# Decay constants made on GpSimd, pair 0 split first, masks beside layer 1, and a new order in pairs 4 to 8 of a fused attention and MLP kernel

## The chip, the cores and the metric

The kernel runs on one core of one Trainium2 chip. The metric is device time in microseconds, taken as the median of the timed runs. Times inside the kernel come from one execution that the hardware profiler recorded; they count from the start of its span.

## The reference

Eight batches of eight heads, 576 tokens, head size 64. Each head is causal attention with a decay that is built from a running sum of `s`. The heads of a batch are then put side by side and go through a two-layer MLP with a hard-swish.

```python
scores = (1/8) * q @ k.T                        # per batch and head, 576 x 576
cum    = cumsum(maximum(s, 0), axis=-1)
bias   = -(cum[:, :, :, None] - cum[:, :, None, :])
scores = where(causal, -1e9, scores + minimum(bias, 0))
attn   = softmax(scores)                        # over the last axis
x      = (attn @ v) -> (8*576, 8*64)            # 4608 tokens x 512
h      = x @ w_in                               # 512 x 2048
out    = (h * clip(h + 3, 0, 6) / 6) @ w_out    # 2048 x 512, float32
```

## The kernel before

**Pairs of heads.** The 64 heads are worked in 32 pairs; four pairs are a batch. A pair's q and k are cast to float16 and transposed into `qT` and `kT`, three slots deep (`NS = 3`, slot is pair modulo 3). Rows 0 to 63 hold the head dimension. Rows 64 to 67 hold the decay: the running sum split in three float16 parts (high, middle, low) on the k side, and its negative on the q side, with ones across from them. So one matmul gives scores and decay together. The remaining rows of a slot, up to 127, hold constant mask rows, which are written once per slot. They make the later pairs' scores causal at a coarse grain.

**Batch 0 (pairs 0 to 3, `FIRST = 4`)** has a start-up path of its own. `first_columns` takes `s` in 128 pieces of 64 tokens, scans each (`scan`), and lets TensorE add up the pieces with two selection matrices, `sums`, which are loaded from DRAM. The split parts go straight into the spare columns of `x0`, a tile of q and k rows in float16, and `turn_first` transposes 68 columns at once. `scores_half` computes half of a head's scores over all 128 rows and adds the triangle with matmuls on `ident` and `tri`. `keep_warm` issues matmuls that compute nothing. The mask rows of slot 0 are made by `affine_select` on GpSimd and copied into slots 1 and 2 by VectorE (`mask_rows`), all within batch 0.

**Layer 1 of block 0.** The MLP works in nine blocks of 512 tokens. `m1` is the first layer (four matmuls of 512 columns for each of 16 f tiles, then ScalarE and VectorE), `m2` the second (four parts of four matmuls for each of four token tiles t4). While layer 1 of block 0 runs, `decay_scan` and `decay_rows` make the decay rows for all other heads. `store_aug` writes them to DRAM scratch and `load_aug` brings a pair's four rows into its slot of `qT` and `kT`.

**The queue of SP.** Nearly all loads are issued by SP, in program order. Pair 4's loads (`load_nine`, contiguous rows) stand behind a small transfer, `fence`, which reads from a part of `w_out`. So they are not issued before that part of `w_out` has landed:

```python
nc.sync.dma_start(out=fence_dram, in_=w_out_sb[0:1, 7, 0:32])
load_nine(FIRST)
```

`w_out` is loaded in four quarters of four f rows each by GpSimd's queue; row 7 is in the second quarter. Then come the loads of pairs 5 and 6, each with its aug rows.

**Layer 2 of block 0 beside pairs 4 to 8.** The 16 parts of `m2(0, ...)` are the list `fill`. Some are run before pair 4's transposes (`turn_nine`); the others are handed out, one at each `more()`, inside `second_pair`, which writes out the order of a pair's scores (`s0`, `s1`, four banks for each head), values (`v`, in two groups) and transposes by hand. From pair 9 on, `weave` mixes attention and MLP tasks by weights.

**PSUM.** Banks 0 to 2 are a ring for scores ("S"), which `x_transpose` also uses; 3 and 4 a ring for the MLP, with transposes in 3; 5 the ring "Y"; 6 and 7 hold attention outputs.

Engines run their own queues in program order. The schedule is manual: what stands first in the program is issued first on its engine.

Of the kernel before, what the change touches and what calls it, by code (L numbers as in the profile page):

```python
# [16 lines left out]
def kernel(  # L17
# [49 lines left out]
    def pair_of_banks(b):  # L67
# [4 lines left out]
    NG = COLS * W2 // 64  # L72
    g = np.arange(128)
    sel_np = g[:, None] == g[None, :NG]
    low_np = (g[:, None] < g[None, :NG]) & (g[:, None] // 9 == g[None, :NG] // 9)
    sums_dram = nc.inline_tensor(
        np.ascontiguousarray(
            np.stack([m[:, k::2] for k in range(2) for m in (sel_np, low_np)], axis=1)
        ).astype(np.float32),
        name="sums",  # L80
    )

    PARTS = [(2 * FIRST, 14), (14, 20), (20, 32), (32, 48), (48, NH)]
# [19 lines left out]
    warm = cpool.tile([128, 512], F16, tag="c_warm")  # L103
    one = cpool.tile([128, 2], F16, tag="c_one")
    keep = cpool.tile([128, 64], F16, tag="c_keep")
# [13 lines left out]
    s_first = work.tile([128, 64], F32, tag="s_first", bufs=1)  # L119
    sums = work.tile([128, 4, NG // 2], F32, tag="sums", bufs=1)  # L120
    scan = work.tile([128, 64], F32, tag="scan", bufs=1)
# [30 lines left out]
    def mask_view(sl, i):  # L152
        return (kT, qT)[i][64:128, sl, 0:W2].rearrange("p (h t) -> p h t", h=2)

    nc.vector.memset(warm, 0.0)
    nc.vector.memset(one[:, 0:1], 1.0)
    nc.vector.memset(x0[:, :, :, 0, D:D + 3], 1.0)
    nc.vector.memset(x0[:, :, :, 1, D + 3:D + 4], 1.0)
    both = [[0, 2], [1, SEQ]]
    select(  # L160
        mask_view(0, 1), both, 4 * GRAN, -GRAN, -16384.0,
        warm[64:128, 0:1].unsqueeze(1).to_broadcast([64, 2, SEQ]),
    )
    select(ident, [[1, 128]], 0, -1, 0.0, one[:, 0:1].to_broadcast([128, 128]))
    select(ident, [[-1, 128]], 0, 1, 0.0)

    def key_rows():
        nc.vector.memset(one[:, 1:2], 1.0)
        k_rows = mask_view(0, 0)
        select(  # L170
            k_rows, both, 4 * GRAN, -GRAN, 0.0,
            one[64:128, 1:2].unsqueeze(1).to_broadcast([64, 2, SEQ]),
        )
        select(k_rows, [[0, 2], [-1, SEQ]], -4 * GRAN + GRAN - 1, GRAN, 0.0)
        select(tri, [[1, 128]], 0, -1, -65504.0, warm[:, 0:128])

    def more_pads():
        nc.gpsimd.memset(kT[:, :, W2:W2 + 64], 0.0)
        nc.gpsimd.memset(v_f[64:128, :, :, 4, :], 0.0)
        nc.gpsimd.memset(v_h[:, :, :, :, D:VW], 1.0)  # L180
        nc.gpsimd.memset(Pm[:, :, 1600:PW], 1.0)
        select(keep, [[1, 64]], 0, -1, 0.0, one[:, 0:1].to_broadcast([128, 64]))

    def mask_rows(sl, i):
        nc.vector.tensor_copy(out=mask_view(sl, i), in_=mask_view(0, i))

# [217 lines left out]
    def scores_half(hd, half):  # L404
        p, hh = hd // 2, hd % 2
        sl = p % NS
        off = hh * SEQ
        b, p0, parts, masks = HALVES[half]
        S = pair_of_banks(b)
        ops = []  # L410
        for kt, lo, hi, c in parts:
            ops.append((
                c, hi - lo, kT[:, sl, off + 128 * kt:off + 128 * (kt + 1)],
                qT[:, sl, off + lo:off + hi],
            ))
        for c, n in masks:
            ops.append((c, n, ident, tri[:, 0:n]))
        ops.sort(key=lambda o: o[0] // 512)
        for i, (c, n, lhsT, rhs) in enumerate(ops):
            bk = c // 512  # L420
            nc.tensor.matmul(  # L421
                out=S[:, c:c + n], lhsT=lhsT, rhs=rhs,
                start=(i == 0 or ops[i - 1][0] // 512 != bk),
                stop=(i == len(ops) - 1 or ops[i + 1][0] // 512 != bk),
            )
        n = max(c + n for c, n, _, _ in ops)
        nc.scalar.activation(  # L427
            out=Pm[:, hd % NS, p0:p0 + n], in_=S[:, 0:n], func=AF.Exp, scale=0.125, bias=0.0
        )
# [245 lines left out]
    def second_pair(p, fill):  # L675
# [9 lines left out]
        if first:  # L685
            run(s0[2:3])
            cast_qk(p + 1)
            more()
        else:
            transpose_group(p, 1)  # L690
            before = values(2 * p - 1)
            run(before[0] + s0[2:3] + before[1])
            if p in (FIRST + 2, FIRST + 4):
                m2_result(0, (p - FIRST) // 2)
        run(s0[3:])
        if first:
            more()
            mask_late()
            run(s1[:3])
            transpose_group(p + 1, 0)  # L700
            mask_late()
            run(v[0] + v[1] + s1[3:])
        else:
            cast_qk(p + 1)
            mask_late()
            run(s1[:2])
            more()
            x_transpose(p - 1)
            run(s1[2:3] + v[0] + s1[3:])
            transpose_group(p + 1, 0)  # L710
            mask_late()
            run(v[1])
        load_aug(p + 3, nc.sync)
# [66 lines left out]
    def first_columns():  # L780
# [5 lines left out]
        )  # L786
        key_rows()
        cT = PS[:, 7, 0:NG // 2]
        for half in range(2):
            o = cT[64 * half:64 * half + 64, :]  # L790
            nc.tensor.matmul(
                out=o, lhsT=scan, rhs=sums[:, 2 * half, :], start=True, stop=False
            )
            nc.tensor.matmul(
                out=o, lhsT=scan[:, 63:64].to_broadcast([128, 64]), rhs=sums[:, 2 * half + 1, :],
                start=False, stop=True,
            )
        c3 = cT.rearrange("p (a t) -> p a t", a=COLS)
        r3 = rest.rearrange("p (a t) -> p a t", a=COLS)
        hi, mid, lo = (x0[:, :, :, 1, D + j] for j in range(3))  # L800
        nc.vector.tensor_copy(out=hi, in_=c3)
        nc.scalar.activation(out=x0[:, :, :, 0, D + 3], in_=hi, func=AF.Copy, scale=-1.0)
        nc.vector.tensor_tensor(out=r3, in0=c3, in1=hi, op=ALU.subtract)
# [3 lines left out]
    def cast_first(p, i, t0, t1, copy):  # L807
        copy(out=x0[:, p, t0:t1, i, 0:D], in_=qk_f[p][:, t0:t1, i, :])

    def turn_first(p, i, t0, t1, b, copy):  # L810
        pT = f16(pair_of_banks(b) if (t1 - t0) > 8 else PS[:, b, :], (t1 - t0) * 128)
        for t in range(t0, t1):
            c = (t - t0) * 128
            nc.tensor.matmul(
                out=pT[0:XW, c:c + 128], lhsT=x0[:, p, t, i, :], rhs=ident,
                is_transpose=True, start=(c % 1024 == 0),
                stop=(t == t1 - 1 or c % 1024 == 896),
            )
        dst = (qT, kT)[i]
# [6 lines left out]
    load_part(0, 0, 0, 5, A)  # L826
    A.dma_start(out=sums, in_=sums_dram.ap())
    load_part(0, 1, 0, 5, nc.sync)
# [7 lines left out]

    keep_warm(7)
    cast_first(0, 0, 0, 5, A.copy)
    cast_first(0, 1, 0, 5, A.copy)
    first_columns()  # L840
    keep_warm(2)
    turn_first(0, 0, 0, 5, 4, A.copy)
    turn_first(0, 1, 0, 5, 5, V.tensor_copy)
    cast_first(0, 0, 5, 9, G.tensor_copy)
    cast_first(0, 1, 5, 9, G.tensor_copy)
    mask_rows(1, 1)
    keep_warm(1)
# [11 lines left out]
    for hd in range(2 * FIRST):  # L859
        p, odd = hd // 2, hd % 2  # L860
        scores_half(hd, 0)
        if hd == 0:
            turn_first(0, 0, 5, 9, 6, V.tensor_copy)
            turn_first(0, 1, 5, 9, 7, V.tensor_copy)
            mask_rows(1, 0)
        if not odd:
            if p == 0:
                cast_pair(1)
                more_pads()
            if p == 2:  # L870
# [12 lines left out]
        elif p + 1 < FIRST:  # L883
            turn_first(p + 1, 1, 0, 9, 4, V.tensor_copy)
            if p + 2 < FIRST:
                cast_pair(p + 2)
        scores_half(hd, 1)
        if hd > 0:
            attend(hd - 1)
        if hd == 1:  # L890
            for i in range(2):
                mask_rows(2, i)
        if odd and p > 0:
# [19 lines left out]
    store_aug(0)  # L913
    nc.sync.dma_start(out=fence_dram, in_=w_out_sb[0:1, 7, 0:32])
    load_nine(FIRST)
    load_aug(FIRST, nc.sync)
    load_v(FIRST, nc.sync)
    for p in range(FIRST + 1, FIRST + 3):
        load_pair(p)
        load_aug(p, nc.sync)  # L920
    store_aug(1)
    run(m1_0[5:14])
    m2_of = {n: m2_tasks(n) for n in range(NBLK)}
    run(m1_0[14:])
    cast_nine(FIRST)
    cast_v(FIRST)
    parts = [(0, 0), (0, 1), (0, 2), (1, 0), (1, 1), (0, 3), (1, 2), (1, 3)]
    parts += [(t4, part) for t4 in (2, 3) for part in range(4)]
    fill = [(lambda t4=t4, part=part: m2(0, t4, part, t4 == 3), 1.0) for t4, part in parts]
    run(fill[:3])  # L930
    turn_nine(FIRST, 6)
    run(fill[3:6])
    m2_result(0, 0)
    fill = fill[6:]
    second_pair(FIRST, fill)
    for p in range(FIRST + 1, PXD + 1):
        second_pair(p, fill)
    ph = PS[:, 4, :]
    m1_sum(1, 0, ph, range(KC - 1))
    transpose_group(PXD + 1, 1)  # L940
    m1_sum(1, 0, ph, range(KC - 1, KC))
    m1_act(1, 0, ph)
    def weighted(m1s, m2s):
        return [(task, 0.85) for task, _ in m1s] + [(task, 1.3) for task, _ in m2s]

    weave(att_of[0], weighted(m1_tasks(1)[1:], m2_of[1][:12]))
    second = weighted([], m2_of[1][12:]) + weighted(m1_tasks(2), m2_of[2][:8])
# [39 lines left out]
```

## Time and profile before

| what | value |
|---|---|
| timed runs | 355.48, 355.26, 352.92 us; median 355.26 us |
| profiled execution, its own time | 352.95 us |
| profiled execution, its span | 351.2 us |
| PE busy | 342.0 us (97%) |
| DVE, ACT, POOL busy | 203.2, 207.0, 147.2 us |
| DMA | 53.99 MB, mean 154 GB/s |
| granted TensorE clock | 1.00 |

PE is TensorE, DVE VectorE, ACT ScalarE, POOL GpSimd, SP SyncE; PEld is the load of weights into TensorE. A line of the timeline gives the start, the duration, the engine, the line of the program, the operation, output <- inputs, and in brackets how long the engine had been idle and who released it. A line of the chain gives start, duration and what it was. Matmul ends are modelled: a 512-column matmul is recorded with 379 ns, while one follows the other by 216 ns.

### The profile page before, as it was taken

The page shows a single profiled execution, that of the slowest core. Times are in us where ns is not written, and L with a number is a line of the kernel's source. Part 1 is how long each engine was busy: PE and PEld are TensorE (multiplying, and loading weights), DVE is VectorE, ACT ScalarE, POOL GpSimd, SP SyncE. Part 2 cuts the span into 40 slices and gives each one's busy share as a digit, 9 for nine tenths or more (in the row PEclk, how much of TensorE's full clock was granted, in tenths as well). Part 3 has the DMA queues.
Part 4 walks back from the last instruction along what each step waited for, and adds up shares of the span by engine and source line. Part 5 has one row for each costly group of instructions (what it writes and reads, how often), then busy time and mean ns, then how long its engine had stood idle before and what let it go on. Part 6 is the DMA issues. An engine that isn't in the chain of part 4 may idle for free.

```text
span 351.2 us, 7616 instructions
## 1 busy us (share of the span) xinstructions
PE 342.0 (97%) x2797; PEld 199.3 (57%) x2797; DVE 203.2 (58%) x367; ACT 207.0 (59%) x392; POOL 147.2 (42%) x318
## 2 busy tenths in 40 slices
PE   7999799999999999999999999999999999999996
PEld 3775366666555655555555555555565545444444
DVE  3758567887635883566546644756365635644531
ACT  3776547678655885777467755775577615534410
POOL 7884157654556455545545444444444200000000
PEclk9999999999999999999999999999999999999999
DMA  8999999999999988988897789787923110010012
GB/s 180 240 164 215 220 214 209 199 243 183 175 197 233 207 169 185 210 196 135 200 197 169 157 185 209 151 175 171 219 40 84 49 60 32 17 45 30 30 60 91
DMA packets 160415, 53.99 MB, mean 154 GB/s; under 512 B 152410, under 2 KB 154266, under 8 KB 160378
## 3 DMA queue, kind: packets, MB, share of 16 engines
q1 hardware_dynamic: 157178, 48.68, 63.1%
q0 software_dynamic: 2256, 4.46, 6.8%
q8 instruction: 22, 0.36, 0.5%
q10 hardware_dynamic: 944, 0.37, 0.4%
q14 instruction: 15, 0.12, 0.1%
HBM read 37.47 MB, written 9.95 MB: 135 GB/s over the span
## 4 chain that ended last, share of the span: by engine, by line
PE 85%; DMA 8%; SPq 2%; POOL 2%; DVE 1%; ACT 1%; issue 0%; POOLq 0%
PE PS L565 34%; PE PS L522 31%; PE PS L346 11%; PE PS L443 7%; DMA w_out_sb<-in_moe_w_out_dram 4%; DMA qkf<-in_k_dram 3%; DMA v_f<-in_v_dram 1%; PE PS L591 1%; SPq L200 1%; PE PS L297 1%; DVE qkT L312 1%; ACT Pm L353 1%; POOL v_h L294 1%; SPq L214 0%; SPq L881 0%
## 5 line engine op out<-in xcount | busy, mean ns | idle before, releaser
L522 PE MATMUL PS<-xT,w_in 128*128 128x512 f16 x576 | 142.3, 379 | 0.0
L533 DVE SCALAR_TENSOR_TENSOR gT<-trl,PS 128x512 f16<-128x512 f32 x144 | 97.8, 686 | 76.8 <-ACT trl L532 76.4
L532 ACT ACTIVATE trl<-PS,bias 128x512 f32<-128x512 f32 x144 | 98.8, 693 | 72.7 <-PE PS L522 72.1
L565 PE MATMUL PS<-w_out_sb,gT 128*128 128x512 f16 x560 | 138.7, 379 | 0.0
L353 ACT ACTIVATE Pm<-PS 128x384 f16<-128x384 f32 x224 | 101.5, 509 | 46.8 <-PE PS L346 44.0
L358 POOL TENSOR_SCALAR_AFFINE_SELECT Pm<-Pm 128x64 f16<-128x64 f16 (+2 forms) x214 | 70.6, 333 | 112.4 <-ACT Pm L353 103.3
L522 PEld LDWEIGHTS <-w_in 128*128 128x128 f16 x576 | 60.4, 114 | 44.2 <-issue 0.2
L565 PEld LDWEIGHTS <-gT 128*128 128x128 f16 x560 | 51.0, 98 | 48.5
L346 PE MATMUL PS<-qkT 128*128 128x256 f16 x392 | 61.7, 261 | 1.2 <-DVE qkT L312 0.7
L346 PEld LDWEIGHTS <-qkT 128*128 128x128 f16 x392 | 35.9, 98 | 30.3 <-DVE qkT L312 3.4
L443 PEld LDWEIGHTS <-Pm 128*128 128x128 f16 x960 | 37.7, 97 | 11.1
L443 PE MATMUL PS<-v_h,Pm 128*128 128x65 f16 x960 | 41.0, 193 | 0.0
L580 DVE TENSOR_SCALAR osb<-PS 128x512 f32<-128x512 f32 x34 | 23.4, 688 | 28.5 <-PE PS L565 28.5
L460 DVE TENSOR_TENSOR xs<-PS,r 128x640 f16<-128x640 f32 (+1 forms) x37 | 27.2, 734 | 1.3
L278 POOL CAST xb<-qkf 128x1152 f16<-128x1152 f32 x22 | 25.5, 1159 | 0.0
L294 POOL CAST v_h<-v_f 128x640 f16<-128x640 f32 x32 | 24.0, 750 | 1.9 <-DMA v_f<-in_v_dram 1.9
L427 ACT ACTIVATE Pm<-PS 128x896 f16<-128x896 f32 (+1 forms) x16 | 13.1, 836 | 4.4 <-PE PS L421 4.4
L289 DVE COPY qkT<-turned 64x1152 f16<-64x1152 f16 x22 | 10.6, 482 | 7.1 <-DMA turned<-xb 7.1
L459 DVE RECIPROCAL r<-PS 128x10 f32<-128x10 f32 (+1 forms) x37 | 7.8, 211 | 7.9 <-PE PS L443 7.3
L290 DVE COPY qkT<-turned 64x1152 f16<-64x1152 f16 x22 | 10.9, 496 | 0.3
L312 DVE COPY qkT<-PS 64x640 f16<-64x640 f16 (+1 forms) x20 | 9.1, 453 | 2.8 <-PE PS L297 2.7
L421 PE MATMUL PS<-qkT 128*128 128x64 f16 (+4 forms) x48 | 9.0, 277 | 0.6 <-DVE qkT L820 0.4
(71 smaller groups left out, 112.5 us busy)
## 6 DMA issues: line engine op xcount, KB each, us to landing
out_dram<-osb SPq DMA_DIRECT2D x35, 256.0 KB, 2.8
qkf<-in_q_dram SPq DMA_DIRECT2D x31, 288.0 KB, 3.5
qkf<-in_k_dram SPq DMA_DIRECT2D x31, 288.0 KB, 4.2
v_f<-in_v_dram SPq DMA_DIRECT2D x62, 128.0 KB, 3.3
w_out_sb<-in_moe_w_out_dram POOLq DMA_DIRECT2D x4, 512.0 KB, 15.8
v_f<-in_v_dram SPq DMA_DIRECT2D x32, 32.0 KB, 2.8
w_in<-in_moe_w_in_dram POOLq DMA_DIRECT2D x2, 512.0 KB, 7.3
w_in<-in_moe_w_in_dram POOLq DMA_DIRECT2D x1, 1024.0 KB, 11.9
```

Source lines behind the costliest of these rows:

```text
L278: nc.gpsimd.tensor_copy(out=xb[:, p % 2], in_=qk_f.pop(p))
L294: nc.gpsimd.tensor_copy(out=v_h[:, sl, :, :, 0:D], in_=v_f[:, sl])
L346: nc.tensor.matmul(out=S[:, c:c + hi - lo], lhsT=kT[:, sl, off + 128 * kt:off + 128 * (kt + 1)], rhs=qT[:, sl, off + lo:off + hi], start=( ...
L353: nc.scalar.activation(out=P[:, p0:p0 + n], in_=S[:, 0:n], func=AF.Exp, scale=0.125, bias=0.0)
L358: nc.gpsimd.affine_select(out=view, in_=view, pattern=pattern, compare_op=ALU.is_ge, fill=0.0, base=0, channel_multiplier=-1,)
L443: nc.tensor.matmul(out=O[:, hh, qt * VW:qt * VW + D + 1], lhsT=P[:, c:c + 128], rhs=v_h[:, sl, hh, kt, 0:D + 1], start=(qt == 0), stop=(qt ...
L460: nc.vector.tensor_tensor(out=x_tiles[p].rearrange("p t h d -> p h t d")[:, heads], in0=Ov[:, :, :, 0:D], in1=r[:, 0:n].to_broadcast([128, ...
L522: nc.tensor.matmul(out=ph, lhsT=w_in_t[f // 4][:, kc, f % 4, :], rhs=xT[:, kc, n * 512:(n + 1) * 512], start=(kc == 0), stop=(kc == KC - 1),)
L532: nc.scalar.activation(out=trl, in_=ph, func=AF.Relu, bias=bias3[:, 0:1], scale=1.0)
L533: nc.vector.scalar_tensor_tensor(out=gT2[:, n % 2, f, :], in0=trl, scalar=6.0, in1=ph, op0=ALU.min, op1=ALU.mult)
L565: nc.tensor.matmul(out=po, lhsT=gT2[:, n % 2, f, t4 * 128:(t4 + 1) * 128], rhs=w_out_sb[:, f, :], start=(f == 0), stop=(f == NF - 1),)
L580: nc.vector.tensor_scalar_mul(out=osb, in0=pouts[n, t4], scalar1=1.0 / 6.0)
```

## The change

It has five parts.

- `sums` is no longer loaded; GpSimd makes it in four selects from a tile of float32 ones. GpSimd makes its own ones, and VectorE takes over the memsets of paddings.
- Pair 0 gets tiles of its own: `q0`, `k0`, and `dec0` for the decay columns of k. `split_of` splits pair 0's nine columns first and those of pairs 1 to 3 later. The k side of pair 0 is transposed in two groups, 64 columns of k and 4 of decay.
- The scores of batch 0 run over 68 rows, so mask rows are not needed there. They are made after `decay_rows`, by GpSimd in slot 2 and by a GpSimd copy into slot 1; ScalarE copies them into slot 0.
- The fence reads a row of the third quarter of `w_out`. The aug loads of pairs 5 and 6 stand behind all loads of pairs 5 and 6 and the second store of decay rows.
- In layer 2, five parts run before `turn_nine` and two after it (before: three and three). Inside a pair the parts and scores change places, and the sums of two f tiles of block 1 are started early in banks 4 and 5.

The core of the diff:

```diff
-    A.dma_start(out=sums, in_=sums_dram.ap())
+    sel, low = sums[:, 0], sums[:, 1].rearrange("p (a b) -> p a b", b=9)
+    nh = NG // 9
+    select(low, [[9, nh], [1, 9]], -1, -1, 0.0, one_f.unsqueeze(1).to_broadcast([128, nh, 9]))
+    select(low, [[-9, nh], [0, 9]], 0, 1, 0.0)
+    select(sel, [[1, NG]], 0, -1, 0.0, one_f.to_broadcast([128, NG]))
+    select(sel, [[-1, NG]], 0, 1, 0.0)
...
+    def make_masks():
+        q_rows, k_rows = mask_view(MADE, 1), mask_view(MADE, 0)
...
+        for i in (1, 0):
+            nc.gpsimd.tensor_copy(out=mask_view(FIRST % NS, i), in_=mask_view(MADE, i))
...
     def mask_rows(sl, i):
-        nc.vector.tensor_copy(out=mask_view(sl, i), in_=mask_view(0, i))
+        nc.scalar.copy(out=mask_view(sl, i), in_=mask_view(MADE, i))
...
-                c, hi - lo, kT[:, sl, off + 128 * kt:off + 128 * (kt + 1)],
-                qT[:, sl, off + lo:off + hi],
+                c, hi - lo, kT[0:XW, sl, off + 128 * kt:off + 128 * (kt + 1)],
+                qT[0:XW, sl, off + lo:off + hi],
...
-            if p in (FIRST + 2, FIRST + 4):
-                m2_result(0, (p - FIRST) // 2)
+            if p in (FIRST + 1, FIRST + 2):
+                m2_result(0, p - FIRST)
...
             mask_late()
+            more()
             run(s1[:2])
-            more()
             x_transpose(p - 1)
-            run(s1[2:3] + v[0] + s1[3:])
+            run(v[0] + s1[2:3])
             transpose_group(p + 1, 0)
             mask_late()
-            run(v[1])
+            run(s1[3:] + v[1])
...
+    def split_of(cT, a0, a1):
+        n = a1 - a0
...
+            hi, mid, lo = (dec0[:, :, j].unsqueeze(1) for j in range(3))
+            minus = q0[:, :, D + 3].unsqueeze(1)
         nc.vector.tensor_copy(out=hi, in_=c3)
-        nc.scalar.activation(out=x0[:, :, :, 0, D + 3], in_=hi, func=AF.Copy, scale=-1.0)
+        nc.vector.tensor_scalar_mul(out=minus, in0=hi, scalar1=-1.0)
...
-    keep_warm(7)
+    keep_warm(5)
...
-    first_columns()
-    keep_warm(2)
+    sums_of = first_columns()
+    split_of(sums_of, 0, 1)
+    keep_warm(1)
...
-            turn_first(0, 1, 5, 9, 7, V.tensor_copy)
-            mask_rows(1, 0)
+            turn_first(0, 1, 5, 9, 5, V.tensor_copy)
...
-            turn_first(p + 1, 1, 0, 9, 4, V.tensor_copy)
+            turn_first(p + 1, 1, 0, 9, 6 if p == 0 else 4, V.tensor_copy)
...
+    make_masks()
-    nc.sync.dma_start(out=fence_dram, in_=w_out_sb[0:1, 7, 0:32])
+    nc.sync.dma_start(out=fence_dram, in_=w_out_sb[0:1, 11, 0:32])
...
     for p in range(FIRST + 1, FIRST + 3):
         load_pair(p)
-        load_aug(p, nc.sync)
     store_aug(1)
...
+    for i in (1, 0):
+        mask_rows((FIRST + 2) % NS, i)
+    for p in range(FIRST + 1, FIRST + 3):
+        load_aug(p, nc.sync)
...
-    run(fill[:3])
+    run(fill[:5])
     turn_nine(FIRST, 6)
-    run(fill[3:6])
+    run(fill[5:7])
     m2_result(0, 0)
-    fill = fill[6:]
+    early = [m1_sum_early(f) for f in range(2)]
+    fill = fill[7:] + early
```

## The prediction

> **What bounds the kernel now.** I read the page first (busy shares, slices), then the chain of waits, the waits by length, and timelines of the stages that the diff touches.
>
> ```profile
> PE 342.0 (97%) x2797; PEld 199.3 (57%) x2797; DVE 203.2 (58%) x367; ACT 207.0 (59%) x392; POOL 147.2 (42%) x318
> DMA  8999999999999988988897789787923110010012
> ```
>
> TensorE is busy 342.0 of 351.2 us, and the DMA engines are nearly full for two thirds of the span. No matmul of the main work is removed, so the change can only fill holes in PE: 9.2 us that the page shows, plus short stalls that the modelled ends of matmuls cover. The chain says what ends last early on:
>
> ```profile
> 15.64 3.63 DMA v_f<-in_v_dram
> ...
> 22.01 14.85 DMA w_out_sb<-in_moe_w_out_dram
> 37.59 5.64 DMA qkf<-in_k_dram
> 44.69 2.59 PE PS L565 x12
> ```
>
> Up to 44 us the end is set by data, not by engines: pair loads, the second quarter of w_out (landed 36.86), then pair 4's q and k (landed 43.23), whose issue stands behind the fence on that quarter. From 44.69 on the chain is PE. Three kinds of hole lie in the changed stages, by the timeline:
>
> ```profile
> 4.88 0.44 PE L791 MATMUL PS<-sums,scan 128*64 128x36 f32 x4 [0.45 <-DMA sums<-sums]
> 16.32 0.67 POOL L808 CAST gT<-qkf 128x576 f16<-128x576 f32 x1 [0.54 <-DMA qkf<-in_q_dram]
> 19.42 0.72 POOL L294 CAST v_h<-v_f 128x640 f16<-128x640 f32 x1 [0.39 <-DMA v_f<-in_v_dram]
> 44.02 0.68 PE L297 MATMUL PS<-idtri,t 128*128 128x128 f16 x9 [1.90 <-POOL t L255]
> 58.99 0.28 PEld L346 LDWEIGHTS <-qkT 128*128 128x128 f16 x4 [0.53 <-DVE qkT L312]
> ```
>
> First, the decay columns wait for the constants `sums` until 4.88, though `scan` is done at 3.53. The casts of pair 3 and of v of pair 2 wait for their loads. Second, PE waits 1.90 us for pair 4 (42.1 to 44.0). Third, in pairs 5 to 8, the first score of the second head waits for the copies out of the second transpose group, about half a microsecond each time.
>
> **What the Trainium skill says.** "DMA: Bandwidth & Descriptors", section "Issuing engines are not separate DMA queues": transfers issued from different engines run on the same 16 DMA engines and interleave. The trace agrees: pair 4's k needs 5.64 us while the w_out stream runs, against a median of 4.2 us for k loads. Its section "Queues, rings and completion order": within a ring, descriptors are consumed in order, so a small load issued late stands behind the large ones before it; the trace records no landing for the aug loads, since nothing waited for one. "TensorE: Matmul & The Clock Gate", section "LDWEIGHTS (loading the stationary operand)": a weight load's time goes by columns, not by contraction rows. So scores over 68 rows instead of 128 gain nothing on PE. The trace has 98 ns for 128 columns at every score; no run yet shows fewer rows.
>
> **The change part by part.**
>
> *Constants by GpSimd, pair 0 split first.* A select of 64x1152 takes 1154 ns and one of 128x128 takes 296, so about 0.84 ns per element: 0.25 us for 72 columns. Float32 is not shown; I bound it at 0.5. Four of them from about 1.0 put `sums` at 2.0 (at most 3.0), before the scan's 3.53. DVE's added memsets (0.09 to 0.47 each, mostly under 0.2, by their like) fit before s_first lands at 3.0. The sum matmuls then start at 3.6, not 4.88. DVE starts 0.77 after them, at 4.4 (as 5.65 follows 4.88); five small operations (0.32, about 0.2, 0.21, 0.28, 0.32) end at 5.75. Five transposes of `dec0` (0.5) and a copy (0.49) give the first score at 6.9 instead of 8.06: PE is 1.15 us earlier. Nine extra transposes (about 0.06 each, 0.5 us) are in this; three warm matmuls go. Using banks 6 and 7 for pair 1's k also removes a 0.46 us wait.
>
> How much of it lasts? Pair 3's q cast waits for its load and ends at 16.99; its transposes run at 17.47. So the lead falls to 0.5 us there. v of pair 2 is cast at 20.14, and attention uses it at 20.31: the lead falls to 0.2. The removed 72 KB of `sums` may bring the loads 0.3 us earlier (72 KB at the 230 GB/s of that stage). I carry 0.3 us to the end of batch 0; the bounds are 0 and 1.2.
>
> *Masks beside layer 1.* Four DVE copies of mask rows (0.46 to 0.65) leave batch 0. POOL gets three selects (3 x 1.15), two copies (about 1.15 each, like the cast of 1152 elements) and `keep` after its decay rows, that is from 34.3 to about 40.5; it was idle until pair 4's cast at 42.57. ACT gets two copies (about 1.1 each by the estimate from its 1152 columns) after 40.26; it was idle until 47.48. Both are covered: 0. Without that cover pair 4's aug load would be late; it waited until 41.34 anyway, for the store of the decay rows.
>
> *The fence moves one quarter on, turning pair 4 moves behind five fills instead of three.* The issues of w_out begin at 21.48, 22.01, 22.57 and 23.1. With the view's 12.9, 15.8 (median) and 18.8 us to landing and 36.86 for the second, the landings are 34.4, 36.9, 39.3 and 41.9. Pair 4's loads are thus issued at 39.6, not 37.17. They do not lose 2.4 us: most of the bytes moved only when the stream ended. From 41.9 to 43.23 the old kernel had about half of the 576 KB left; now about three quarters are left, some 0.6 us more. I take a k landing of 43.7 (43.2 to 44.5). Cast 0.7, transposes 0.7 and hand-overs put the end of the turn at 45.15, against 44.70. But PE has then done five fills of 0.86 us instead of three: 1.73 - 0.45 = 1.3 us gained. If the transfers behave as the stream alone allows, 0.5 to 1.7. One part of it is at risk: bank 4 is needed for a fill about 3.3 us after the turn, while DVE frees it at 3.75 (four copies, 3.11, and the result's 0.67): 0.5 us, hidden by what follows.
>
> *The aug loads of pairs 5 and 6 go behind all loads of pairs 5 and 6 and a store.* This is the step that I hold against the change. SP's timeline before:
>
> ```profile
> 47.03 0.43 SPq L227 DMA_DIRECT2D qkT<-aug_scratch  x1
> 47.50 0.37 SPq L200 DMA_DIRECT2D qkf<-in_q_dram  x1
> 47.91 0.61 SPq L200 DMA_DIRECT2D qkf<-in_k_dram  x1
> 48.62 1.55 SPq L214 DMA_DIRECT2D v_f<-in_v_dram  x2
> 50.22 0.61 SPq L218 DMA_DIRECT2D v_f<-in_v_dram  x1
> 50.93 0.71 SPq L227 DMA_DIRECT2D qkT<-aug_scratch  x1
> 51.69 0.29 SPq L617 DMA_DIRECT2D aug_scratch<-aug  x1
> ```
>
> Pair 5's aug load leaves at 47.03; now it is passed by q, k and three v loads of pair 6 and the store. Take out its 0.47, add the store's 0.34: it leaves at 50.7. A landing takes 2.8 us (median of the small v loads just ahead of it in the ring; bounds 2.2, s_first with little ahead, and 4.4, the longest q load seen). So pair 5's rows are there at 53.5 (52.5 to 55.5). Pair 5's first score waits for them, and PE runs in order: all fills, values and transposes are queued behind. PE would otherwise be there at 45.15 + 6.3 (the old 7.2 from turn to pair 5, less one fill) + 0.5 = 51.9. It idles 1.6 us. In all, pair 5 starts at 53.5 with ten fills done; before, it started at 51.89 with nine. 53.5 - 51.89 - 0.86: a loss of 0.75 us, with everything gained further up swallowed. ACT and DVE idle with PE there.
>
> *Order within pairs 5 to 8.* The fill of 0.86 us moves between the last score of the first head and the first of the second, which now covers the DVE copies. By the timeline, PE's hole there was 0.37, 0.46, 0.49 and 0.49: 1.8 us. What is late next is the exponent: the third score of the second head needs its bank back from ACT. With 0.48 and 0.59 us for the two exponents, and 0.28 of transposes and 0.20 of values between, I find about 0.18 us of new waiting per pair. 1.8 - 0.7 = 1.1 us gained (0.4 to 1.8). Two sums of block 1 begin early in banks 4 and 5: the same matmuls, and the 0.16 us wait at the last transposes goes. 0.2 gained.
>
> Sum: +0.75 - 1.1 - 0.2 = -0.55 us in the span. After 76 us nothing but small shifts in the weaving order changes; I give them 0 (+-0.3). From 351.2 this is 350.65; with the 1.75 us outside the span of the profiled execution (352.95), 352.4. The timed runs lie on two levels: 352.92, and 355.26 and 355.48, with the profiled one on the lower. The median is 2.3 us above my base. I make the sum against the mean of the four, 354.15, and get 353.6, rather than choose a level.
>
> **The rivals.**
>
> A, *the aug load is in time.* If small loads land in 1.2 us or SP gets ahead of the old times (pair 4's aug load leaves earlier because no pair load stands around its store), the 1.6 us of idling goes. Then -0.55 - 1.6 - 0.3 of start-up lead = -2.45 to -3.2: 350.9 to 351.7 from the mean. For it: nothing waited for an aug load before, so its latency may be shorter. Against: 18 KB behind 590 KB in the same ring.
>
> B, *slower: the aug load decides by more.* SP slips by the 0.6 us that pair 4's loads come later, and landing takes 4.4: 55.7, thus +2.95 - 1.3 = +1.65: 355.8. It decides from a landing of 54.05 on, where the loss equals the gains of the pairs. For it: the DMA share is 1.12 between 44.7 and 51.9. Against: the share is 0.61 between 41.3 and 44, so the late loads can catch up.
>
> C, *the early lead lasts.* If the loads follow PE's lead (fewer transfers ahead, w_in and w_out streams start 1 us earlier), pair 4 and the aug load move up by 1 us too, and the whole is -4: 350.2. The waits of 0.54 and 0.39 us on loads at full DMA speak against it.
>
> **How the numbers follow.** Forecast 0.55, A 0.2, B 0.17, C 0.08. The range goes from C's end, and a little below it for the lower level, to B's on the upper level: 349.5 to 357.3. About 1% (3.5 us) is what this measurement can tell from no change; the forecast, most of A and of B lie within it. Faster by more needs C, or A with the levels in its favour: 0.2. Slower by more needs B and the upper level: 0.12. Same: 0.68.
>
> **What would show it.** Right: first score near 6.9; `sums` no releaser of PE; PE's wait for pair 4 under 1.9 us with five fills ahead; a wait of PE on the DMA of qkT's aug rows of 1 to 2 us at pair 5; pairs 5 to 8 at about 5.1 us each instead of 5.4. Wrong: no such wait, a constant select over 0.5 us, or exponents that stall PE in pairs 5 to 8 by more than 0.4 us each.

## The result, and the profile after

The changed kernel takes 355.18 us (median of 20 runs, 353.2 to 356.5), the kernel before 353.02 us on the same chip (20 runs, 352.44 to 355.48). The ratio is 1.0037, with a 95% interval of 1.0019 to 1.0054: about 1.3 us slower. The medians differ by more, 2.16 us: executions of one kernel spread over some 3 us even at a granted clock of 1.00, so the ratio, which lies close to that of the means (354.94 and 353.60 us), is the better measure, and one profiled execution shows where time goes but not the mean loss. The forecast was 0.55 us in the other direction. The time lies within 1% of no change, but its direction was wrong.

The profiled execution of the changed kernel took 355.25 us with a span of 353.5 us, against 352.95 and 351.2 before. From its page, the busy row and then the rows of TensorE's clock and of DMA by fortieths of the span:

```profile
PE 343.8 (97%) x2803; PEld 200.9 (57%) x2803; DVE 201.2 (57%) x373; ACT 209.5 (59%) x393; POOL 149.4 (42%) x322
...
PEclk9999998999999999999999999999999999999999
DMA  8999899998999898987997889778933110010012
```

PE is busy for 1.8 us more than before with the same large matmuls. Most of that is in the seventh digit of the clock row (53 to 62 us), which was a 9 before. The timeline of PE in the changed kernel (start, duration, instruction, in brackets its idle time and what ended it) shows what became of the holes of before:

```profile
3.59 0.44 PE L795 MATMUL PS<-sums,scan 128*64 128x36 f32 x4
...
6.98 0.39 PE L425 MATMUL PS<-qkT 68*128 68x512 f16 x1 [0.26 <-DVE qkT L841]
...
20.36 0.62 PE L447 MATMUL PS<-v_h,Pm 128*128 128x65 f16 x15 [0.17 <-POOL v_h L298]
...
43.69 0.68 PE L301 MATMUL PS<-idtri,t 128*128 128x128 f16 x9
...
53.92 0.90 PE L350 MATMUL PS<-qkT 128*128 128x256 f16 x4 [2.47 <-DMA qkT<-aug_scratch]
...
76.80 1.02 PE L526 MATMUL PS<-xT,w_in 128*128 128x512 f16 x4 [0.80 <-DVE qkT L316]
```

The first three lines are the start: the sum matmuls no longer wait for constants, the first score comes at 6.98 instead of 8.06, and by 20.36 (20.31 before) the lead is gone. Most of it goes early: the first values come at 11.79, against 12.01 before. The wait of 1.90 us at pair 4's transposes has gone too. In its place PE idles 2.47 us ahead of pair 5, and 0.80 us after pair 8.

The chain of waits points to the same place (start, length, link):

```profile
49.37 1.50 ACT Pm L357 x4
50.87 2.92 DMA qkT<-aug_scratch
53.78 0.14 issue
53.92 0.90 PE PS L350 x4
```

The aug rows of pairs 5 and 6 are issued at 50.87 and land 2.92 us later. The windows of the changed kernel over that stage (window, length, busy time of each engine with its instructions, granted clock, DMA share, GB/s) show what follows:

```profile
52.00:54.00 2.00, 0.08 (x1) 0.11 (x2) 0.00 (x0) 0.00 (x0) 0.09 (x1) 0.87 0.57 160
54.00:58.00 4.00, 4.00 (x36) 2.90 (x36) 2.38 (x6) 1.99 (x5) 1.50 (x4) 0.64 1.06 223
58.00:61.00 3.00, 3.00 (x46) 2.32 (x44) 2.43 (x7) 2.12 (x5) 2.29 (x6) 1.00 0.95 217
```

In the first window every engine stands almost still. In the second the granted clock is 0.64, so PE is full for 4 us and does 2.6 us of work.

The starts of pairs 5 to 9 locate the loss of the profiled execution. A pair starts at its first score (the first group of 128x256 matmuls), all in us.

| kernel | pair 5 | 6 | 7 | 8 | 9 | span |
|---|---|---|---|---|---|---|
| before | 51.89 | 57.16 | 62.55 | 67.97 | 76.13 | 351.2 |
| changed | 53.92 | 60.27 | 65.23 | 70.18 | 78.98 | 353.5 |

These points are not quite at equal work. At pair 5 the changed kernel has one fill more behind it (four matmuls of 0.22 us, 0.87 us in all), and at pair 9 one column group of the first product more, again 0.87 us. Corrected, it is 53.92 - 51.89 - 0.87 = 1.17 us late at pair 5, and 78.98 - 76.13 - 0.87 = 1.98 us late at pair 9. Of the 2.3 us in the span, 2.0 exist by then.

### The profile page after: what moved, and what is told of

It reads as the page before. It is cut to its first block, busy times and chain, and to the rows that moved or that the text cites. A ratio compares the mean times of both kernels' runs of the same rounds, so it can differ in the third digit from the quotient of the medians.

```text
span 353.5 us, 7629 instructions
## 1 busy us (share of the span) xinstructions
PE 343.8 (97%) x2803; PEld 200.9 (57%) x2803; DVE 201.2 (57%) x373; ACT 209.5 (59%) x393; POOL 149.4 (42%) x322
## 4 chain that ended last, share of the span: by engine, by line
PE 89%; SPq 4%; DMA 2%; DVE 2%; ACT 1%; issue 1%; POOL 1%; POOLq 0%; ACTq 0%
PE PS L526 35%; PE PS L569 33%; PE PS L350 11%; PE PS L447 7%; SPq L204 2%; SPq L218 2%; DMA v_f<-in_v_dram 1%; PE PS L595 1%; DVE qkT L274 1%; DMA qkT<-aug_scratch 1%; PE PS L301 1%; ACT Pm L357 1%; PE PS L489 1%; PE PS L425 1%; DVE qkT L316 0%
## 5 line engine op out<-in xcount | busy, mean ns | idle before, releaser
L362 POOL TENSOR_SCALAR_AFFINE_SELECT Pm<-Pm 128x64 f16<-128x64 f16 (+2 forms) x214 | 71.4, 336 | 114.9 <-ACT Pm L357 105.3
L425 PE MATMUL PS<-qkT 68*128 68x64 f16 (+4 forms) x48 | 9.1, 277 | 0.4 <-DVE qkT L841 0.3
```

The source lines that it names most:

```text
L362: nc.gpsimd.affine_select(out=view, in_=view, pattern=pattern, compare_op=ALU.is_ge, fill=0.0, base=0, channel_multiplier=-1,)
```

## The experiments

The runs were made on several chips; each ratio is to runs of the kernel before on the same chip. A span, and every time inside a kernel, is that of one profiled execution. The theory was first that three things cost time: the late aug rows, the clock after the hole, and the second early sum. The rivals were that one of them explains everything, or that the order of the pairs or the masks do; the masks were looked at in the trace only.

**Aug rows of pairs 5 and 6 early, all else as changed.** The order of SP's issues is again pair, aug, pair, aug, store:

```
     load_aug(FIRST, nc.sync)
     load_v(FIRST, nc.sync)
-    for p in range(FIRST + 1, FIRST + 3):
-        load_pair(p)
-    store_aug(1)
+    load_pair(FIRST + 1)
...
         mask_rows((FIRST + 2) % NS, i)
-    for p in range(FIRST + 1, FIRST + 3):
-        load_aug(p, nc.sync)
+    load_aug(FIRST + 1, nc.sync)
+    load_pair(FIRST + 2)
+    load_aug(FIRST + 2, nc.sync)
+    store_aug(1)
```

> The changed kernel with one thing put back: pair 5's aug load is issued before pair 6's loads, and pair 6's before the second store, as in the kernel before. Theory 1 (the aug load of pair 5, queued behind pair 6's loads, stops PE at pair 5 and lets its clock drop): pair 5's first score starts near 51.3 instead of 53.9, the clock stays at 1.0 between 52 and 58 us (0.72 in the changed kernel), pair 5 lasts about 5.0 us instead of 6.5, and the whole is 3.5 to 4.2 us under the changed kernel, some 351.2 against 355.2 and 353.0 before. Theory 2 (the loss comes from the early sums of block 1 and what follows pair 8): at most 1 us is gained. Theory 3 (the two kernels only sit on different ones of two levels of run time, 2.3 us apart): the runs still spread over 353.5 and 355.5.

Measured: 353.3 us against 353.98, ratio 0.9974 (0.9943 to 1.0005), span 351.5. It was run again later:

> The changed kernel with only the aug loads of pairs 5 and 6 early again, as the partner of the kernel with both edits on one chip. Theory (the aug wait and the dropped clock cost about 2 us of span): 1.5 to 2.5 us under the changed kernel, ratio to before 0.996 to 0.999. Rival (most of the loss is the second early sum's): under 1 us below the changed kernel, ratio 1.001 or more.

Measured: 352.73 us against 354.23, ratio 0.9959 (0.9939 to 0.9979), span 351.0. Against the changed kernel's 1.0037 the two are 0.6 and 0.8% lower, 2.2 to 2.8 us. That is less than the 3.5 to 4.2 us of the first theory, and more than the second allows. The third fails as the whole cause, since the ratio moves although the runs still spread (351.23 to 355.27 us). The hole and the low clock are gone, as the windows of the first run show:

```profile
52.00:54.00 2.00, 2.00 (x31) 1.41 (x29) 1.70 (x5) 1.69 (x4) 1.38 (x4) 1.00 0.76 188
54.00:58.00 4.00, 4.00 (x63) 3.23 (x62) 3.58 (x11) 2.70 (x7) 3.28 (x8) 1.00 0.92 211
```

Pair 5 starts at 51.76 and 51.22 in the two, and lasts 4.95 and 4.96 us. So the late rows turn a change that is worth 0.3 to 0.4% into a loss of 0.4% (the first of the two intervals just includes no gain).

**The kernel before with late aug rows only.**

```
     for p in range(FIRST + 1, FIRST + 3):
         load_pair(p)
-        load_aug(p, nc.sync)
     store_aug(1)
+    for p in range(FIRST + 1, FIRST + 3):
+        load_aug(p, nc.sync)
```

> The kernel before with only that one step of the change: the aug loads of pairs 5 and 6 go behind all loads of pairs 5 and 6 and the second store. Theory 1: pair 5's first score moves from 51.9 to about 54, the clock drops if PE's idle time is near 2.9 us or longer, and the whole is 2 us slower without a clock drop, 3.3 us with one. Theories 2 and 3: no change beyond 0.5 us.

Measured: 355.33 us against 353.98, ratio 1.0071 (1.0036 to 1.0106), or 2.5 us (1.3 to 3.8; the medians differ by 1.35). The same wait appears, first by PE's timeline and then by the chain:

```profile
54.33 0.54 PE L346 MATMUL PS<-qkT 128*128 128x256 f16 x4 [1.93 <-DMA qkT<-aug_scratch]
```

```profile
51.37 2.82 DMA qkT<-aug_scratch
```

The window of 54 to 58 us has a clock of 0.68. Taking the late rows out of the changed kernel gives back 2.2 or 2.8 us, and putting them into the kernel before costs 2.5 us; within the intervals the two sides agree. The 2.9 us of the expectation is how long the weight loads stood idle in the changed kernel's hole (2.93). It is no threshold: here PE idles for 1.93 us and the weight loads for 2.39, and the clock drops.

**Warm matmuls in the hole.** Ten matmuls on a constant tile, whose result is not used, keep PE busy between pair 4 and pair 5:

```
         more()
+        if first:
+            keep_warm(10)
```

> The changed kernel with ten 512-column matmuls on the constant tile (about 2.2 us, into bank 3, never read) between pair 4's last fill and pair 5's first score, where PE waits for the aug rows anyway. If the clock drop after the wait is real and costs about 1.5 us, pair 5 still starts near 53.9 but lasts 5.0 us instead of 6.5, the clock between 52 and 58 us is 1.0, and the whole is 1.2 to 1.6 us under the changed kernel. If the clock has no part in it, the time is the same or up to 0.3 us longer.

Measured: 354.09 us against 353.98, ratio 1.0008 (0.9988 to 1.0029), span 352.1. The windows of that kernel:

```profile
52.00:54.00 2.00, 2.00 (x13) 1.01 (x12) 0.10 (x1) 0.00 (x0) 0.32 (x1) 1.00 0.53 171
54.00:58.00 4.00, 4.00 (x62) 3.14 (x61) 3.19 (x8) 3.34 (x8) 2.82 (x7) 1.00 0.98 217
```

The wait for the rows is as long (pair 5 starts at 53.67), but the clock stays at 1.00 and pair 5 lasts 4.95 us, not 6.35. In the profiled executions this is 1.40 us. The ratios put it at 0.3%, 1 us, with intervals that just overlap; that is a little less than the 1.2 to 1.6 us expected.

**Only the first early sum, aug rows late.** The sum of block 1's second column group goes back into the weaving:

```
-    early = [m1_sum_early(f) for f in range(2)]
+    early = [m1_sum_early(f) for f in range(1)]
...
-    for f in range(2):
-        m1_sum(1, f, PS[:, 4 + f, :], range(KC - 1, KC))
-        m1_act(1, f, PS[:, 4 + f, :])
+    m1_sum(1, 0, PS[:, 4, :], range(KC - 1, KC))
+    m1_act(1, 0, PS[:, 4, :])
...
-    weave(att_of[0], weighted(m1_tasks(1)[2:], m2_of[1][:12]))
+    weave(att_of[0], weighted(m1_tasks(1)[1:], m2_of[1][:12]))
```

> The changed kernel with only the first of the two early sums (as before); the aug loads of pairs 5 and 6 stay late. It asks what the second early sum costs by itself, in the presence of the aug wait. Theory (cover): the four matmuls of the sum of f = 1 stand again over VectorE's copies out of bank 3, so the wait of 0.8 us after pair 8 and its weight load go, and pair 9's first score comes about 1.3 us earlier than after's 78.98, near 77.7; the hole ahead of pair 5 and the dropped clock stay (granted clock 0.7 to 0.8 at 52 to 58 us). Time 1.2 to 1.8 us under the changed kernel, ratio to before 0.998 to 1.001. Rival (the second sum is free, what was won in the third kernel came from the aug loads alone): the ratio stays at the changed kernel's 1.0037 +-0.002, and pair 9's first score stays at 78.5 to 79.0.

Measured: 353.8 us against 354.23, ratio 1.0004 (0.9985 to 1.0023), span 352.0. Time and ratio fall where the first theory put them, but the trace gives another reason. PE's timeline has the hole and then another wait in place of the one of 0.80 us; the windows follow:

```profile
53.72 0.54 PE L350 MATMUL PS<-qkT 128*128 128x256 f16 x4 [2.48 <-DMA qkT<-aug_scratch]
...
73.58 0.38 PE L301 MATMUL PS<-idtri,t 128*128 128x128 f16 x4 [0.67 <-POOL Pm L362]
```

```profile
52.00:54.00 2.00, 0.28 (x3) 0.28 (x4) 0.00 (x0) 0.00 (x0) 0.00 (x0) 1.00 0.63 177
54.00:58.00 4.00, 4.00 (x62) 3.15 (x60) 3.15 (x8) 3.29 (x8) 2.83 (x7) 1.00 0.89 200
```

PE idles 2.48 us as in the changed kernel, yet the clock does not drop. Pair 9 starts at 76.20, 2.78 us earlier than in the changed kernel: 0.20 from pair 5's start, 1.40 from the clock, 0.87 because one column group less has been done by then, and only 0.31 from pair 8. The wait of 0.80 us goes, and a wait of 0.67 us on GpSimd's masks takes its place. In these two traces, then, the second sum costs 0.31 us at equal work; most of the theory's 1.3 us had been a comparison at unequal work. The ratio fell by 1.2 us all the same (0.3 to 2.1 by the two intervals, taken as independent). That the clock drops more rarely here, which comes below, explains an estimated 0.4 us of it; whether the second sum costs more than 0.31 us in other executions stays open.

**Both edits: aug rows early and one early sum.**

> As the first one (aug loads in the old order), and only the first of the two sums of block 1 is started early; the second one comes after pair 9's second transposes, as before, as cover for VectorE's copies out of bank 3. Theory 2 as the second part of the loss: PE's waits after pair 8 (0.8 us on the copies of the transposes, 0.4 us on the cast) shrink, and it is 0.7 to 1.4 us under the first one. If those waits only move, it is within 0.3 us of the first one.

Measured: 351.55 us (6 runs) against 353.98, ratio 0.9933 (0.9904 to 0.9962), span 350.2. Again, beside the kernel with only the aug rows early:

> The kernel with both edits (aug loads of pairs 5 and 6 early, only the first sum early) again, beside the kernel with the aug loads alone early on the same chip, for a direct comparison. Theory (two costs that add up): 0.5 to 0.7% under before, ratio 0.993 to 0.995, and 1.2 to 1.8 us under the kernel with the aug loads alone. Rival (the lead that the second edit brings is taken away by the transposes that wait for loads): within 0.5 us of the kernel with the aug loads alone, ratio 0.996 to 0.998.

Measured: 352.42 us against 354.23, ratio 0.9957 (0.9926 to 0.9987), span 350.6. The second pair of runs differs by 0.3 us, the first by 1.75. So the second sum's own cost with the rows in time is not settled beyond "between nothing and 1.8 us"; the traces show 0.31 in pair 8. This version beats both kernels, by 0.4 to 0.7% against the kernel before.

The following four change one thing in it, on one chip. This version itself gave 0.9933 on that chip and 0.9957 on another, so a difference of 0.3% among the four is not settled by ratios alone.

**The fence on the old quarter.**

```
-    nc.sync.dma_start(out=fence_dram, in_=w_out_sb[0:1, 11, 0:32])
+    nc.sync.dma_start(out=fence_dram, in_=w_out_sb[0:1, 7, 0:32])
```

> The kernel with the old order of aug loads and one early sum (the fourth of the first set: ratio 0.993 to the kernel before), and the fence back on the second quarter of w_out. If the later fence costs nothing because pair 4's bytes move only when the w_out stream ends (my step), pair 4's transposes end within 0.5 us of the same time, near 44.4, and the total is within 0.3 us. If the issue time decides, they end 1.5 to 2.4 us earlier and PE, with five fills ahead, gains nothing from it, or up to 0.6 us.

Measured: 352.61 us against 354.48, ratio 0.9946 (0.9922 to 0.997), span 351.2. Pair 4's transposes start at 44.13; with the later fence, in nine other traces with five fills ahead and the early start, they start at 43.25 to 45.30 (mean 43.9). At equal work the kernel before is at 44.02 + 1.73 = 45.75. So, by these single traces, the two fills that were moved ahead bring about 1.6 us of it, and the fence a few tenths at most.

**The old order inside pairs 5 to 8.**

```
-            more()
             run(s1[:2])
+            more()
             x_transpose(p - 1)
-            run(v[0] + s1[2:3])
+            run(s1[2:3] + v[0] + s1[3:])
             transpose_group(p + 1, 0)
             mask_late()
-            run(s1[3:] + v[1])
+            run(v[1])
```

> The same base, with the order of work inside pairs 5 to 8 as in the kernel before. If the new order is worth what the trace of the changed kernel shows for pairs 6 and 7 (4.95 us a pair against 5.4), pairs 5 to 8 take 1.6 to 1.9 us longer up to pair 9's first score, and the total grows by 1 us or more. If the lead is lost later anyway to loads (VectorE waits 2.8 us for a transposed load near 91 us, and PE 1.3 us behind it), the total grows by 0.5 us or less.

Measured: 352.7 us against 354.48, ratio 0.9961 (0.994 to 0.9983), span 350.1. Pairs 5 to 8 start at 50.85, 56.11, 61.50 and 66.91 and pair 9 at 74.84: 23.99 us, against 22.48 us with the new order (50.93 to 73.41). The new order does save 1.5 us at pair 9, but in these two executions none of it is left in the span, 350.1 against 350.2. Over all runs it looks different: the ratio with the old order is 0.3% higher (0.9961 against 0.9933), 1.0 us, as the first half of the expectation had it, with intervals that overlap; and the profiled execution with the old order was the fastest of its 20. So how much of the 1.5 us lasts on average is open. What takes it back in the profiled execution is seen in the trace of the kernel with both edits, first SP's timeline, then VectorE's, then PE's:

```profile
76.62 0.44 SPq L231 DMA_DIRECT2D qkT<-aug_scratch  x1
77.16 1.41 SPq L285 DMA_TRANSPOSE turned<-xb  x1
```

```profile
80.60 0.49 DVE L293 COPY qkT<-turned 64x1152 f16<-64x1152 f16 x1 [1.22 <-DMA turned<-xb]
```

```profile
82.75 1.02 PE L526 MATMUL PS<-xT,w_in 128*128 128x512 f16 x4 [1.30 <-DVE gT L537]
```

With the old order SP issues the same transpose no later:

```profile
76.23 0.44 SPq L231 DMA_DIRECT2D qkT<-aug_scratch  x1
76.77 1.41 SPq L285 DMA_TRANSPOSE turned<-xb  x1
```

SP issues its loads one after the other from about 70 to 79 us in both, almost without a pause. The transpose stands behind them, so it does not follow PE's lead. VectorE waits 1.22 us for it, its next products of the MLP wait behind, and PE stops for 1.30 us for a bank. With the old order PE is there later and does not wait. (VectorE's wait of 2.8 us that the expectation names ends at 98.00, and PE does not stop behind it.)

The other traces with early aug rows agree. Six of the eight reach pair 9 between 1.4 and 2.7 us ahead of the kernel before, at equal work. In each of them PE stops once, for 1.25 to 2.41 us, behind VectorE's copies of a transposed load, at 82.75 and 84.03 in two and near 117 in four. The chain of the kernel with only the aug rows early has it thus:

```profile
110.68 3.43 DMA turned<-xb
...
117.08 1.02 PE PS L526 x4
```

The other two, the old order among them, are 0.7 and 1.3 us ahead at pair 9; PE does not stop there, and they keep their lead. How often executions without a trace stop in this way is not known.

**A late start.** Four more warm matmuls ahead of pair 0's transposes.

```
     split_of(sums_of, 0, 1)
-    keep_warm(1)
+    keep_warm(5)
```

> The same base, with four more warm matmuls ahead of the first transposes, so that pair 0's first score comes about 1 to 1.5 us later (near 8.2 instead of 7.0 us). If the lead of the start-up is lost to the loads of pair 3 and of v by 20 us (my step), the time from 24 us on is the same and the total within 0.3 us. If the lead lasts, the total grows by about 1 us.

Measured: 351.62 us against 354.48, ratio 0.9923 (0.9903 to 0.9943). The first score comes at 8.27 instead of 6.91, and the ratio does not rise. But the trace does not show what the expectation gave as the reason: the 1.36 us are not lost by 24 us. In the traces of the two kernels layer 2 starts at 40.38 instead of 39.02, and pair 9 at 74.76 instead of 73.41. So by the ratio the lead of the start is worth nothing, and where it goes is not shown.

**The first result's scaling on ScalarE instead of VectorE.**

```
-        if (n, t4) == (0, 3):
+        if n == 0 and t4 in (0, 3):
```

> The same base, with the first result of layer 2 scaled on ScalarE, which idles there, instead of VectorE, whose four copies for pair 4 stand ahead of it. PE's wait of 0.4 us for bank 4 in pair 4 goes. If PE's time in this stage counts, 0.4 to 0.6 us is gained on the base (ratio near 0.992); if the loads swallow it, nothing.

Measured: 352.66 us against 354.48, ratio 0.9953 (0.993 to 0.9977). The fill that waited 0.37 us for bank 4 no longer waits, and from pair 4's transposes to pair 9 it takes 29.55 us (44.03 to 73.58) instead of 30.07 (43.34 to 73.41). The ratio does not fall below the 0.9933 of the base. In the profiled execution the whole lead goes in PE's stop of 2.41 us at 84.03, behind a VectorE that has waited for a transposed load, like that of the order.

## Why the prediction was wrong

Two terms of the sum failed. The clock after the hole at pair 5 was not in it, and cost 1.40 us in the profiled execution. Pair 8 with the early sums was put at a gain of 0.5 us, and lost 0.64. At equal work, the delays that were predicted and measured up to pair 9 in the profiled execution (us; minus is a gain):

| step | predicted | measured |
|---|---|---|
| start of pair 5 | +0.75 | +1.17 |
| clock in pair 5 | not in the sum | +1.40 |
| order in pairs 5 to 7 | -0.8 | -1.22 |
| pair 8 with the early sums | -0.5 | +0.64 |
| sum | -0.55 | +1.98 |

The measured order is (4.95 - 5.27) + (4.96 - 5.39) + (4.95 - 5.42), with the undisturbed 4.95 for pair 5. The predicted 1.1 is split by the four holes of before (0.37, 0.46, 0.49 and 0.49, each less 0.18), and the 0.2 is added to pair 8. The measured terms add up to 1.99; the 0.01 is rounding.

*Start.* Close at the first score: `sums` at 2.21 (2.0), first score 6.98 (6.9), and the weight loads of 68 rows took 97 ns on average, as those of 128 rows did before. The lead is gone by the attention of pair 2, as predicted, but not for the reason given: it was already down to 0.22 us at the first values, ahead of the loads that were to take it. The late start, whose 1.36 us last to pair 9, speaks against that reason too. The 0.3 us carried did not show: layer 2 starts at 39.33, against 39.37 before.

*Masks beside layer 1.* Right, cost 0: GpSimd ended them at 40.3, and waited 1.95 us for pair 4 after that; ScalarE's two copies ended at 42.45, and it was idle until 46.43.

*Fence and five fills.* The direction was right, the size too small. Predicted was an end of the turn at 45.15, measured is 44.37: a gain of 2.06, not 1.3. The loads of pair 4 did not need the 0.6 us more, GpSimd cast q at 42.26. But the extra 0.8 us only lengthened the wait at pair 5, as the prediction said of the rest.

*Aug rows.* The mechanism was named and is shown from both sides. Issue 50.87 (50.7), landing 53.79 (53.5), nearly as predicted; the idle time was 2.47, not 1.6, half because PE came 0.45 us earlier and half because pair 5 started at 53.92, not 53.5. The failing sentence is "ACT and DVE idle with PE there": it stops at idling. The granted clock after the hole was not considered. In the profiled execution it costs 1.40 us. It does not come each time. One such drop takes 1.7 of 353 us, a mean granted clock of 0.995; that or less was recorded in 8 of 20 executions of the changed kernel, in 3 of 6 of the kernel before with late rows, in 3 of 22 with late rows and one early sum, in 24 of 157 of the kernel before, and in 7 of 134 of the eight runs with early aug rows. The 8 have a median of 355.4 us, the other 12 one of 354.6. Averaged over executions the clock thus explains an estimated 0.35 of the 1.3 us ((8/20 - 24/157) x 1.40); a profile with the drop shows 2.3. On average, then, pair 8, which lasts 8.80 us in all four traces with both early sums, is likely the larger of the two failures.

*Order in pairs 5 to 8.* Right, and better than predicted for pairs 5 to 7: 4.95 us each, against "about 5.1".

*Pair 8.* This step failed. "The same matmuls ... 0.2 gained" overlooked that the fills are a fixed stock. Five instead of three go ahead of pair 4's turn, so pair 8 has none left to lay over its waits: with sixteen large matmuls in both, it lasts 8.80 us against 8.16. With one early sum it is 7.62 + 0.87 = 8.49, so 0.31 of the 0.64 is the second sum's. Even with the old order and one early sum pair 8 takes 7.93 + 0.87 = 8.80, so the order isn't the cause. That the rest, 0.33 us, is the missing fill fits all of these, but was not tried alone.

*After 76 us.* "0 (+-0.3)" held for the kernel as changed (1.98 to 2.3), and in the profiled executions it fails for the kernels with a larger lead. At pair 9 those with early aug rows are ahead of before by 0.7 to 2.7 us at equal work; at the end of the span by 1.1 us at the best, and several by nothing. The ratios of all runs are kinder, 0.9 to 2.7 us, so the spans overstate what is lost. Rival A's -2.45 to -3.2 fails partly at pair 8 and partly after pair 9: with the rows in time the kernel is 1.6 and 2.1 us ahead at pair 9 in its two traces, and gained 0.9 to 1.5 us by the ratios. Rival B's side and nearly its size came true by luck (+1.65; +1.3 by the ratio), but through the clock and pair 8, not through a landing past 54.05.

## What to carry to other kernels

A small load that an in-order engine needs next must not be queued behind large ones: here 2.9 us to landing and some 2.5 us of the whole run hung on its place in SP's queue. A lead can be lost at the next stage bound by transfers, as in six traces here; look at when that stage's transfers are issued before adding up gains ahead of it. Compare two traces only at points where both have done the same work, since a first score that comes 2.8 us earlier may hold 0.9 us less work. And do not judge an edit by the spans of two profiled executions where the runs spread over more than the edit is worth.

## What was not expected of the hardware

Idle times of PE of 2.47 and 1.93 us were enough for the clock to fall, and another of 2.48 us was not. The traces suggest why. In all thirteen the granted clock changes only at multiples of 3.41 us from its first rise: in the changed kernel at 5.69, 53.48 (14 multiples later) and 56.89 us, in the kernel before with late rows at 4.21, 55.41 (15) and 58.82. So the clock seems to be decided at the end of each stretch of 3.41 us, and how a hole lies to these stretches differs from one execution to the next (the first rise comes at 4.16 to 7.31 us). Here are the stretch before the drop and the one after it, first of the changed kernel, then of the kernel before with late rows; last are the two across which the hole of the kernel with late rows and one early sum lies:

```profile
50.07:53.48 3.41, 1.38 (x18) 0.61 (x14) 1.72 (x5) 0.99 (x3) 1.52 (x4) 1.00 0.73 162
53.48:56.89 3.41, 2.97 (x28) 2.30 (x29) 1.27 (x4) 1.71 (x4) 0.70 (x2) 0.50 1.12 244
```

```profile
52.00:55.41 3.41, 1.48 (x23) 1.02 (x22) 0.96 (x3) 0.73 (x3) 1.12 (x3) 1.00 0.69 180
55.41:58.82 3.41, 3.41 (x24) 1.83 (x21) 1.35 (x5) 2.10 (x5) 2.68 (x7) 0.50 0.98 201
```

```profile
48.88:52.30 3.42, 2.36 (x32) 1.51 (x30) 1.76 (x5) 1.69 (x4) 1.85 (x5) 1.00 0.95 192
52.30:55.71 3.41, 1.99 (x29) 1.56 (x30) 1.10 (x4) 1.62 (x4) 0.70 (x2) 1.00 0.80 205
```

By the modelled ends of matmuls, PE idles for 2.03 and 1.93 us of the stretches that a drop follows, and for 1.06 and 1.42 us of the two that share the third hole. In all thirteen traces no other stretch after the first rise and before the last few us has more than 1.73 us of idling, and no other is followed by a drop. A drop is half speed for one whole stretch, 1.7 us of lost clock. Where between 1.73 and 1.93 us the limit lies, and whether it is PE's idle time or something close to it that counts, is not shown.

The Trainium skill, "TensorE: Matmul & The Clock Gate", section "What's actually happening", gives half speed as the throttled state and says that the window of about 3.4 us that decides it runs freely; both agree with these traces. It asks for at least one idle window of that length before the clock falls. Neither hole filled one; the measurement decides, and here some 1.9 us of idling inside one window were enough.
